# A Fourier filter with a sparse mixture of experts: padded first transform, batch 0 in thirds, new issue thresholds, a third list tile

## The chip, the cores and the metric

The kernel runs on one core of a Trainium2 chip. The metric is device microseconds of one execution. The engines are PE (TensorE, with its weight loads shown as PEld), DVE (VectorE), ACT (ScalarE), POOL (GpSimd) and SP (SyncE, which only issues DMA transfers here). ACT and POOL issue transfers too.

## The reference, cut to what matters

```python
X = np.fft.rfft(x, axis=1)                  # x: 8 x 2496 x 256
Yr = Xr @ w_r - Xi @ w_i + b_r              # 256 x 256 weights, on every frequency
Yi = Xr @ w_i + Xi @ w_r + b_i
Y = sign(Y) * max(|Y| - 0.01, 0)            # on real and imaginary part apart
y = np.fft.irfft(Y, n=2496, axis=1)         # 19968 tokens of 256

logits = y @ w_gate                         # 8 experts
expert = argmax(logits); gate = softmax(logits)[expert]
for each expert: keep the 80 tokens with the largest gate
    out[tok] = gate * (relu(y[tok] @ w1[e]) @ w2[e])      # 256 -> 1024 -> 256
all other rows of out are 0
```

The biases are drawn eight times larger than in the listing's distribution; nothing else hangs on that.

## The kernel before

**Transform.** 2496 is taken as 39 x 64. A token index is `64 a + n`, and the first transform (`stageA`) runs over the 39 values of `a`. Three values of `n` share one matmul, so the tile `xt` of loaded input has 39 x 3 = 117 partitions, and the weight `t1s` is a 117 x 117 block matrix (`t1f` is the same in fp32). A batch has six groups `q` of `stageA`, loaded in three chunks. Where `cut` holds, the input is split by `halve` into two fp16 parts `xs` (ACT at L286, POOL at L287) and multiplied at L301. Elsewhere the fp32 input is multiplied directly at L303. Each PSUM result is copied into `zs` as two fp16 parts (ACT at L318, DVE at L319) and stored in DRAM (L325). For batch 0 the store has two halves, 63 and then 54 rows: the first is issued at once and the second waits in the list `second`. Groups 3 to 5 of batch 0 use tiles named `YO` in the place of `zs`.

**Second transform and weights.** `loadZ` (L352) reads z back with another layout, `stageB` (L363 to L365) does the 64-point transform and copies it to `XT` (ACT L368, DVE L369). Stage C (L421) multiplies by the packed weights `WM` of 288 or 337 columns, then comes the soft threshold: ACT's `tp` (L445, or L432 in batch 7), DVE's `R` (L449, or L436), POOL's sums (L452). Then ACT, POOL and DVE make `YT` (L466 and L467, or L495 and L496). After that come the back transforms (L523 and L524 to `YO`, L577 to `hs`) and gate logits `G`.

**Lists.** From the gate values the kernel makes lists of tokens for each expert in three groups `g` (L868 to L915): group 0 and group 1 while the batches run, group 2 at the end. Two int32 tiles hold the lists, `tok` for groups 0 and 2 and `tokb` for group 1. Each is cleared by a memset (L915), filled, and written to the DRAM tensor `cid` (L893). Then rows are gathered, the experts run, and the result is scattered to `out`, which is cleared through the whole run (`out<-zero`, L264).

**Order.** Sixteen steps (batch, column half `ch`) are interleaved: while stage C of one step runs, `doA` puts groups of `stageA` of a later batch and `doB` the `stageB` of the next step in between. A scheduler sets the final order on each engine. `pin` and `keep` keep an instruction's program order, and `tc.issue_after(i)` forbids an instruction to stand ahead of `i`. Every engine then runs its own list strictly in order, so an instruction that waits holds up all behind it. Transfers take one of eight semaphore lanes in turn, and each waits for the previous transfer of its lane.

**Start.** Weights `w_r` and `w_i` come in and `consts` makes `WM` of them (ACT L212, DVE L213 and L214). The biases come by two transfers of 4-byte elements into `bt` (L233), and DVE makes `thr` of them (L235). When the six groups of batch 0 are through, 56 matmuls on zeros (L1376, "warm") stand on PE ahead of `stageB` of step (0, 0).

## Time and profile before

| | |
|---|---|
| three runs | 616.37, 613.64 and 617.41 us; median 616.37 |
| the profiled execution | 613.95 us, of which the span is 612.2 us |
| granted TensorE clock, mean | 0.947 of full speed |
| PE busy | 543.1 us (89%) |
| DVE busy | 400.3 us (65%) |
| POOL busy | 372.4 us (61%) |
| ACT busy | 324.0 us (53%) |
| DMA | 134.98 MB, mean 220 GB/s |

The profiled execution lies 2.4 us under the median of the runs and 0.3 us above the fastest. Times below are microseconds from the start of its span. "Busy" of PE counts matmuls that stand back to back, and a clock of 0.50 in a stretch means that each took twice as long as at 1.00. A row's idle time in brackets is that of its engine just ahead of the row, with what ended it.

### The profile page before, as it was taken

Reading aid. Unit: us, or ns where it says so; the run is one execution under the profiler, and the core shown is the slowest. Engines: PE = TensorE matmul, PEld = TensorE weight load, DVE = VectorE, ACT = ScalarE, POOL = GpSimd, SP = SyncE. Lnnn points to the kernel's source line nnn. Section 1 sums busy time; section 2 is a strip of 40 time slices with the busy share of each in tenths; the row PEclk is TensorE's granted clock in tenths of the full one; section 3 lists DMA queues with packets and bytes.
Section 4 is the critical chain, followed back from the end, with each engine's and each line's share of the span. In section 5 each row is a group of like instructions: output and inputs, shape, how many; then the busy total and the mean of one; then the engine's idle time right before and its main releaser. Section 6 shows DMA issues by size and latency. Waiting matters only on the chain. (4 is left out here: it accounts for less than half of the span.)

```text
span 612.2 us, 12947 instructions
## 1 busy us (share of the span) xinstructions
PE 543.1 (89%) x5059; PEld 396.4 (65%) x5059; DVE 400.3 (65%) x778; ACT 324.0 (53%) x466; POOL 372.4 (61%) x287
## 2 busy tenths in 40 slices
PE   7997599999999999999999859989889978987792
PEld 2464377767677876877786538757757766537692
DVE  3422445666767667666767936788898856846870
ACT  2314657576756656576665426555644547602571
POOL 2005767586867677776777636577752379465671
PEclk9899889999999999999999979989899958987987
DMA  6688697888699798978978884989834859648731
GB/s 191 218 256 202 215 230 237 234 256 239 202 286 257 211 254 253 300 201 242 248 253 235 251 229 90 286 248 283 236 99 117 270 179 319 186 140 281 253 100 32
DMA packets 97218, 134.98 MB, mean 220 GB/s; under 512 B 26547, under 2 KB 78274, under 8 KB 95396
## 3 DMA queue, kind: packets, MB, share of 16 engines
q1 hardware_dynamic: 88517, 113.94, 64.3%
q10 hardware_dynamic: 6506, 10.89, 5.9%
q0 software_dynamic: 2128, 9.25, 4.6%
q8 instruction: 42, 0.69, 0.5%
q14 instruction: 25, 0.20, 0.1%
HBM read 70.74 MB, written 63.31 MB: 219 GB/s over the span
## 5 line engine op out<-in xcount | busy, mean ns | idle before, releaser
L421 PE MATMUL ps<-XT,WM 128*128 128x288 f16 (+4 forms) x1536 | 222.8, 303 | 17.6 <-DVE R L449 12.2
L421 PEld LDWEIGHTS <-WM 128*128 128x128 f16 x1536 | 151.6, 100 | 78.1 <-issue 17.8
L287 POOL TENSOR_TENSOR xs<-xt,xs 117x1024 f16<-117x1024 f32 (+1 forms) x39 | 76.2, 1955 | 43.6 <-ACT xs L286 43.5
L449 DVE SCALAR_TENSOR_TENSOR R<-ps,thr,tp 128x674 f32<-128x674 f32 (+1 forms) x56 | 48.4, 866 | 76.6 <-ACT tp L445 69.7
L467 POOL TENSOR_TENSOR YT<-R,YT 128x1408 f16<-128x1408 f32 (+1 forms) x28 | 73.4, 2620 | 35.4 <-ACT YT L466 30.9
L445 ACT ACTIVATE tp<-ps,thr 128x674 f32<-128x674 f32 (+1 forms) x56 | 43.4, 778 | 85.2 <-PE ps L421 85.2
L452 POOL TENSOR_TENSOR R<-R,sgs 128x576 f32<-128x576 f32 x28 | 35.8, 1280 | 59.4 <-DVE R L449 56.6
L369 DVE TENSOR_TENSOR XT<-ps,XT 128x640 f16<-128x640 f32 (+2 forms) x64 | 51.5, 814 | 22.6 <-ACT XT L368 21.9
L319 DVE TENSOR_TENSOR zs<-ps,zs 117x1024 f16<-117x1024 f32 (+1 forms) x45 | 51.0, 1135 | 21.5 <-ACT zs L318 21.2
L363 PE MATMUL ps<-t2s,z 128*128 128x128 f16 x320 | 57.0, 220 | 6.3 <-DVE XT L369 3.7
L365 PE MATMUL ps<-t2s,z 128*128 128x128 f16 x320 | 57.1, 220 | 0.0
L364 PE MATMUL ps<-t2s,z 128*128 128x128 f16 x320 | 57.1, 220 | 0.0
L368 ACT ACTIVATE XT<-ps 128x640 f16<-128x640 f32 (+2 forms) x64 | 44.4, 701 | 21.8 <-PE ps L365 20.9
L301 PE MATMUL ps<-xs,t1s 117*117 117x512 f16 x213 | 52.6, 381 | 0.8 <-DVE zs L319 0.4
L318 ACT ACTIVATE zs<-ps 117x1024 f16<-117x1024 f32 (+1 forms) x45 | 42.8, 955 | 12.4 <-PE ps L301 6.2
L535 DVE TENSOR_TENSOR YO<-ps,YO 128x768 f16<-128x768 f32 (+1 forms) x50 | 45.3, 907 | 6.0 <-ACT YO L534 6.0
L577 PE MATMUL ps<-YO,vqs 128*128 128x512 f16 (+1 forms) x252 | 48.8, 334 | 0.0
L466 ACT ACTIVATE YT<-R 128x1408 f16<-128x1408 f32 (+1 forms) x28 | 35.4, 1266 | 22.3 <-POOL R L463 20.2
L286 ACT ACTIVATE xs<-xt 117x1024 f16<-117x1024 f32 (+1 forms) x39 | 38.3, 982 | 15.7 <-DMA xt<-in_x 15.7
L523 PE MATMUL ps<-wgi,YT 128*128 128x144 f16 (+1 forms) x302 | 43.5, 229 | 3.3 <-DVE R L449 1.5
L524 PE MATMUL ps<-wgi,YT 128*128 128x136 f16 (+1 forms) x302 | 42.9, 226 | 2.1 <-DVE YT L496 2.1
L534 ACT ACTIVATE YO<-ps 128x768 f16<-128x768 f32 (+1 forms) x50 | 38.6, 775 | 7.5 <-PE ps L524 5.7
(309 smaller groups left out, 1000.4 us busy)
## 6 DMA issues: line engine op xcount, KB each, us to landing
out<-zero SPq DMA_DIRECT2D x48, 384.0 KB
hd<-hs SPq DMA_DIRECT2D x94, 192.0 KB
xt<-in_x SPq DMA_DIRECT2D x44, 312.0 KB
zd<-zs SPq DMA_DIRECT2D x28, 468.0 KB
z<-zd SPq DMA_DIRECT2D x16, 528.0 KB
z<-zd SPq DMA_DIRECT2D x16, 432.0 KB
wt<-in_moe_w ACTq DMA_DIRECT2D x10, 512.0 KB
pair<-in_moe_w SPq DMA_DIRECT2D x8, 512.0 KB
```

The lines of the kernel that those rows point to most:

```text
L287: nc.gpsimd.tensor_tensor(xs[:, 1, :ng], xt[:, j0:j0 + ng], xs[:, 0, :ng], op=ALU.subtract)
L301: nc.tensor.matmul(pt[:117, 512 * j:512 * j + 512], t1s[:, t], xs[:, h, 2 * j:2 * j + 2], start=(i == 0), stop=(i == 2))
L319: nc.vector.tensor_tensor(zs[:, :ng, 1, :], pv[:117, :ng], zs[:, :ng, 0, :], op=ALU.subtract)
L363: nc.tensor.matmul(o, zz(0), t2s[:, cl, 0, :], start=True, stop=False)
L364: nc.tensor.matmul(o, zz(0), t2s[:, cl, 1, :], start=False, stop=False)
L365: nc.tensor.matmul(o, zz(1), t2s[:, cl, 0, :], start=False, stop=True)
L369: nc.vector.tensor_tensor(ov(1), pv, ov(0), op=ALU.subtract)
L421: nc.tensor.matmul(pt[:, o:o + e - a], WM[:, dh, m, wh, 128 * eh:128 * eh + 128], XT[:, dh, xh, c, a:e], start=(i == 0), stop=(i == len(te ...
L449: nc.vector.scalar_tensor_tensor(fv(Rf), pv, thr[:, eh, ri, 1:2], fv(t), op0=ALU.add, op1=ALU.min)
L467: nc.gpsimd.tensor_tensor(yv(1), rv, yv(0), op=ALU.subtract)
L535: dvs.append(nc.vector.tensor_tensor(yol, yy, yoh, op=ALU.subtract))
L577: nc.tensor.matmul(o, tab[:, v], yo(h), start=(i == 0), stop=(i == 2))
```

## The change

1. **Padding.** `t1` gets zero columns, so that the first transform gives 128 rows, with the two halves at 0 to 63 and 64 to 127. All tiles and stores of z have 64 or 128 rows for 63, 54 or 117.
2. **Batch 0.** The input chunks of batch 0 are thirds of `n`, and its z lies in three DRAM tiles. The first third of z is read back after group 3; the rest as before after the last group. The first input chunk of batch 1 is loaded by ACT's queue after group 1, where SP's queue loaded it after the second stores. 44 warm matmuls stand where 56 stood.
3. **Biases.** They are loaded as four rows of 128, transposed on PE, and `thr` is made from PSUM.
4. **Thresholds.** The operations that make `WM` are kept behind the last copies of z of batch 0. `halve` is kept behind the third last (batches 0 and 1) or the last (group (2, 0)) of the ACT instructions listed in `evA`, which are the copies of `stageA` and `stageB` and the `tp` of stage C. A new `split` is called behind the `doB` of the first step.
5. **Batch 7.** The memset of 30 PSUM columns stands behind ACT's `tp`, where it stood ahead of it.
6. **Lists.** Group 2 has a tile of its own, `tokc`.

```diff
-        "t1": split(np.kron(Fw[:, ROWS], np.eye(3)), 1),
+        "t1": split(np.insert(np.kron(Fw[:, ROWS], np.eye(3)), [63] + [117] * 10, 0.0, 1), 1),
-    zd = [[(dr.tile([k, 48, 512], F16, ...), dr.tile([k, 18, 512], F16, ...)) for c, k in enumerate(ZROWS if b == 0 else (39,))] for b in range(B)]
+    zd = [[[dr.tile([r, n, 512], F16, ...) for i, n in enumerate((8, 8, 6) if b == 0 else (16, 6))] for c, r in enumerate((64, 64) if b == 0 else (128,))] for b in range(B)]
...
     def consts():
-        for m, wt in enumerate(wraw):
-            nc.scalar.activation(WM[:, :, m, 0, :], wt, AF.Copy, scale=WS)
-            nc.vector.scalar_tensor_tensor(WM[:, :, m, 1, :], wt, WS, WM[:, :, m, 0, :], op0=ALU.mult, op1=ALU.subtract)
-        nc.vector.tensor_scalar(WM[:, :, 2], WM[:, :, 1], -1.0, None, op0=ALU.mult)
+        with tc.issue_after(evA[-1].ins), tc.issue_after(evD[-1].ins):
+            for m, wt in enumerate(wraw):
+                nc.scalar.activation(WM[:, :, m, 0, :], wt, AF.Copy, scale=WS)
+                nc.vector.scalar_tensor_tensor(WM[:, :, m, 1, :], wt, WS, WM[:, :, m, 0, :], op0=ALU.mult, op1=ALU.subtract)
+            nc.vector.tensor_scalar(WM[:, :, 2], WM[:, :, 1], -1.0, None, op0=ALU.mult)
...
+        bt = wkc.tile([4, 128], F32, name="bt")
         for r, bb in enumerate((b_r, b_i)):
-            bt = wkc.tile([128, 2], F32, name="bt", bufs=2)
-            nc.gpsimd.dma_start(bt, bb.rearrange("(h p) -> p h", p=128))
+            nc.gpsimd.dma_start(bt[2 * r:2 * r + 2], bb.rearrange("(h p) -> h p", p=128))
+        pt = psum()
+        nc.tensor.transpose(pt[:, 0:4], bt, ident[:4, :4])
...
-        nc.scalar.activation(xs[:, 0, :ng], xt[:, j0:j0 + ng], AF.Copy)
+        with tc.issue_after(evA[-3 if b < 2 else -1].ins) if b < 2 or (b, q) == (2, 0) else ExitStack():
+            nc.scalar.activation(xs[:, 0, :ng], xt[:, j0:j0 + ng], AF.Copy)
...
-        for i in parts:
-            p, e, m = ((0, 96, 48), (96, 128, 16))[i]
+        pieces = ((0, 48, 24), (48, 96, 24), (96, 128, 16)) if b == 0 else ((0, 96, 48), (96, 128, 16))
+        for i in parts or range(len(pieces)):
+            p, e, m = pieces[i]
...
-            if c0:
-                nc.vector.memset(pw[:, :c0], 0.0)
             acts.append(nc.scalar.activation(t[:, c0:], pw[:, c0:], AF.Relu, bias=thr[:, eh, ri, 0:1]))
+            if c0:
+                nc.vector.memset(pw[:, :c0], 0.0)
...
-        tok = const.tile([128, 2, 8, 4], I32, name="tokb" if g == 1 else "tok")
+        tok = const.tile([128, 2, 8, 4], I32, name=("tok", "tokb", "tokc")[g])
         nc.vector.memset(tok, 0)
...
+        if q == 1:
+            x1 = loadX(1, 0, None, (A_, A_, A_))
+        if q == 3:
+            z2 = loadZ(0, 0, None, (0,), False)
+    loadZ(0, 0, z2, (1, 2))
     pt = psum()
-    for _ in range(56):
+    for _ in range(44):
...
-            doC(0, 0); doC(0, 1); doA(); doC(1, 0); doA(); doC(1, 1); doA(4)
+            doC(0, 0); doC(0, 1); doA(); doC(1, 0); doA(); doC(1, 1); doA(4, False)
             for _ in Bl:
                 doB()
+            split()
```

How the change moves instructions is shown at three places. The first is **ACT from the last copies of batch 0's second transform on**, in the first step: `xs` is `halve`'s copy, `tp` the soft threshold's, `zs` and `XT` the copies of the first and second transform. Before:

```order
L368 ACTIVATE XT_185<-ps 128x2x320 x2
L286 ACTIVATE xs<-xt 117x1024 x2
L445 ACTIVATE tp_141<-ps,thr 128x674
L445 ACTIVATE tp_142<-ps,thr 128x674
L318 ACTIVATE zs<-ps 117x4x256
L445 ACTIVATE tp_141<-ps,thr 128x674
L466 ACTIVATE YT_435<-R 128x1408
L318 ACTIVATE zs<-ps 117x4x256
L445 ACTIVATE tp_142<-ps,thr 128x674
L318 ACTIVATE zs<-ps 117x4x256 x2
L286 ACTIVATE xs<-xt 117x512
```

After, the same stretch:

```order
L378 ACTIVATE XT_186<-ps 128x2x320 x2
L455 ACTIVATE tp_143<-ps,thr 128x674
L455 ACTIVATE tp_144<-ps,thr 128x674
L324 ACTIVATE zs<-ps 128x4x256
L455 ACTIVATE tp_143<-ps,thr 128x674
L477 ACTIVATE YT_428<-R 128x1408
L324 ACTIVATE zs<-ps 128x4x256
L290 ACTIVATE xs<-xt 117x1024
L455 ACTIVATE tp_144<-ps,thr 128x674
L290 ACTIVATE xs<-xt 117x1024
L324 ACTIVATE zs<-ps 128x4x256 x2
```

The two large `xs` copies have moved from ahead of all four `tp` to behind the third and behind the fourth. Some rows further on, the `xs` of group (2, 0) has moved from ahead of the first `XT` copy of the next step to behind all four of them.

The second place is **DVE just behind the last entries of the lists of group 0** (`G` is a sum of gate logits, `waits` names the queues that a row waits for; DMAHW is a transfer's lane). Before:

```order
L319 TENSOR_TENSOR zs<-ps,zs 117x4x256 [waits DMAHW7_49,Activation_49]
L629 TENSOR_REDUCE G<-Gs 128x160 [waits DVE_49]
L915 MEMSET tok 128x64 [waits DMAHW5_49,DVE_49]
L449 SCALAR_TENSOR_TENSOR R<-ps,thr,tp_142 128x674 [waits Activation_49]
L632 TENSOR_TENSOR gp<-G,gp 128x160 [waits Activation_49]
L319 TENSOR_TENSOR zs<-ps,zs 117x4x256 [waits DMAHW0_49,Activation_49]
```

After:

```order
L325 TENSOR_TENSOR zs<-ps,zs 128x4x256 [waits DMAHW3_49,Activation_49]
L640 TENSOR_REDUCE G<-Gs 128x160 [waits DVE_49]
L460 SCALAR_TENSOR_TENSOR R<-ps,thr,tp_144 128x674 [waits Activation_49]
L643 TENSOR_TENSOR gp<-G,gp 128x160 [waits Activation_49]
L325 TENSOR_TENSOR zs<-ps,zs 128x4x256 [waits DMAHW4_49,Activation_49]
```

The memset of the list tile, with its wait for a transfer, has gone from this place; the clearing of `tokc` stands at the start of DVE's list.

The third place is **SP's queue from the first stores of z on**, in batch 0 (`z_229` and `z_221` are the tiles that the second transform reads; the names of the DRAM tiles are `zd` and `ze` before, and `z_84` to `z_89` after). Before:

```order
L325 DMA zd_84<-zs 63x2048 x3
L325 DMA zd_84<-YO_212 63x2048
L325 DMA ze_85<-YO_212 63x2048
L325 DMA ze_85<-YO_224 63x1024
L352 DMA z_229<-zd_84 48x11x512 x2
L352 DMA z_229<-ze_85 16x11x512 x2
L325 DMA zd_86<-zs 54x2048 x3
L325 DMA zd_86<-YO_212 54x2048
L325 DMA ze_87<-YO_212 54x2048
L325 DMA ze_87<-YO_224 54x1024
L276 DMA xt<-in_x 39x2048 x6
```

After:

```order
L332 DMA z_84<-zs 64x2048 x2
L332 DMA z_85<-zs 64x2048
L362 DMA z_221<-z_84 24x11x512 x2
L332 DMA z_85<-YO_217 64x2048
L332 DMA z_86<-YO_217 64x2048
L332 DMA z_86<-YO_232 64x1024
L362 DMA z_221<-z_85 24x11x512 x2
L362 DMA z_221<-z_86 16x11x512 x2
L332 DMA z_87<-zs 64x2048 x2
L332 DMA z_88<-zs 64x2048
L332 DMA z_88<-YO_217 64x2048
L332 DMA z_89<-YO_217 64x2048
```

Two loads of the first third now stand between the third and the fourth store, and three of the six `xt` loads have left this queue for ACT's, where they stand between the copies to `zs` of groups 1 and 2.

## Rows read from the trace of the kernel before

**Rows 1.** The page's first part: busy time and share of the span, PE.

```profile
PE 543.1 (89%) x5059; PEld 396.4 (65%) x5059; DVE 400.3 (65%) x778; ACT 324.0 (53%) x466; POOL 372.4 (61%) x287
```

**Rows 2.** Stretches of the span, in microseconds: each row has the stretch and its length, the busy time of each engine with its instructions, the granted TensorE clock, the busy share of the DMA engines and GB/s.

```profile
28.00:35.00 7.00, 6.31 (x31) 2.73 (x29) 0.00 (x0) 0.00 (x0) 0.00 (x0) 1.00 0.92 245
...
76.00:80.00 4.00, 3.88 (x18) 2.46 (x18) 1.96 (x4) 1.62 (x3) 3.86 (x2) 0.50 0.79 283
...
96.00:340.00 244.00, 240.40 (x2247) 180.59 (x2245) 169.79 (x260) 157.97 (x219) 176.94 (x136) 1.00 0.84 245
...
354.00:362.00 8.00, 1.26 (x9) 0.70 (x8) 1.10 (x4) 2.89 (x4) 0.04 (x1) 0.88 0.95 256
362.00:366.00 4.00, 4.00 (x18) 2.42 (x18) 2.11 (x3) 0.00 (x0) 3.92 (x3) 0.50 0.47 154
...
485.00:508.00 23.00, 17.61 (x152) 13.80 (x149) 16.34 (x35) 9.73 (x13) 14.21 (x7) 0.63 0.74 229
508.00:540.00 32.00, 27.54 (x154) 17.27 (x151) 24.02 (x96) 19.71 (x26) 19.46 (x10) 0.95 0.72 223
```

**Rows 3.** The timeline of PE over the start: start, length, operation and tiles, count, and in brackets the idle time ahead of it with what ended it.

```profile
10.05 1.95 PE L303 MATMUL ps<-xt,t1f 117*117 117x512 f32 x4 [0.44 <-DMA XT<-in_x]
14.21 5.39 PE L303 MATMUL ps<-xt,t1f 117*117 117x512 f32 x8 [2.21 <-DMA xt<-in_x]
...
22.01 12.25 PE L1376 MATMUL ps<-z 128*128 128x512 f16 x56
34.95 0.22 PE L363 MATMUL ps<-t2s,z 128*128 128x128 f16 x1 [0.69 <-DMA z<-ze]
```

**Rows 4.** The timeline of DVE, over the last copies of batch 0's first transform.

```profile
21.97 0.68 DVE L213 SCALAR_TENSOR_TENSOR WM<-tp,WM 128x512 f16<-128x512 f32 x1
...
23.71 0.42 DVE L214 TENSOR_SCALAR WM<-WM 128x1024 f16<-128x1024 f16 x1
24.04 0.68 DVE L319 TENSOR_TENSOR YO<-ps,YO 117x512 f16<-117x512 f32 x1
```

**Rows 5.** The timeline of ACT there. The first row is the copy of group 2, the second those of groups 4 and 5.

```profile
16.91 1.02 ACT L318 ACTIVATE zs<-ps 117x1024 f16<-117x1024 f32 x1 [1.18 <-PE ps L303]
...
21.35 1.51 ACT L318 ACTIVATE YO<-ps 117x1024 f16<-117x1024 f32 x2
```

**Rows 6.** The timeline of SP: start and length of the issues of transfers.

```profile
25.20 1.36 SPq L352 DMA_DIRECT2D z<-zd  x2
27.57 1.22 SPq L352 DMA_DIRECT2D z<-ze  x2
...
34.30 5.97 SPq L276 DMA_DIRECT2D xt<-in_x  x6
```

**Rows 7.** Transfers issued between 8 and 36 us: tiles, queue, count, and KB of each.

```profile
z<-zd SPq DMA_DIRECT2D x2, 528.0 KB
...
z<-ze SPq DMA_DIRECT2D x2, 176.0 KB
```

**Rows 8.** The timeline of ACT in the first step.

```profile
47.91 1.06 ACT L286 ACTIVATE xs<-xt 117x1024 f16<-117x1024 f32 x1 [8.38 <-DMA xt<-in_x]
51.94 1.06 ACT L286 ACTIVATE xs<-xt 117x1024 f16<-117x1024 f32 x1 [2.97 <-DMA xt<-in_x]
52.90 1.52 ACT L445 ACTIVATE tp<-ps,thr 128x674 f32<-128x674 f32 x2
...
71.70 1.06 ACT L286 ACTIVATE xs<-xt 117x1024 f16<-117x1024 f32 x1 [3.87 <-DMA xt<-in_x]
72.67 0.69 ACT L368 ACTIVATE XT<-ps 128x640 f16<-128x640 f32 x1
```

**Rows 9.** The timeline of DVE in the first step.

```profile
53.74 1.75 DVE L449 SCALAR_TENSOR_TENSOR R<-ps,thr,tp 128x674 f32<-128x674 f32 x2 [13.32 <-ACT tp L445]
```

**Rows 10.** The timeline of PE in the first step.

```profile
54.71 1.97 PE L303 MATMUL ps<-xt,t1f 117*117 117x512 f32 x4 [3.54 <-DVE R L449]
...
69.14 0.22 PE L363 MATMUL ps<-t2s,z 128*128 128x128 f16 x1 [1.47 <-DVE zs L319]
...
74.26 0.26 PE L363 MATMUL ps<-t2s,z 128*128 128x128 f16 x1 [3.68 <-DVE XT L369]
```

**Rows 11.** The timeline of DVE behind the lists of group 0.

```profile
360.96 0.11 DVE L915 MEMSET tok<- 128x64 int32 x1 [6.90 <-DMA cid<-tok]
```

**Rows 12.** The timeline of PE: 24 matmuls of stage C with 288 columns, in an undisturbed place and behind that wait.

```profile
132.75 3.10 PE L421 MATMUL ps<-XT,WM 128*128 128x288 f16 x24
...
361.93 5.53 PE L421 MATMUL ps<-XT,WM 128*128 128x288 f16 x24 [6.74 <-DVE R L449]
```

**Rows 13.** The timeline of SP ahead of that wait.

```profile
353.61 1.27 SPq L352 DMA_DIRECT2D z<-ze  x2
354.97 0.54 SPq L893 DMA_DIRECT2D cid<-tok  x1
```

**Rows 14.** The timeline of ACT in batch 7.

```profile
490.53 1.06 ACT L826 ACTIVATE pair<-pair 128x1024 f16<-128x1024 f32 x1 [4.68 <-DMA pair<-in_moe_w]
491.49 1.36 ACT L495 ACTIVATE YT<-R 128x1408 f16<-128x1408 f32 x1
```

**Rows 15.** The waits from 430 to 500 us: engine and line, what it waited for, microseconds in all, times, the longest.

```profile
ACT tp L432 <- DVE ps L431: 9.4, 3, 3.9
...
DVE R L436 <- ACT tp L432: 1.2, 2, 0.9
```

More of the change, by code (lines that the diff above doesn't have):

```diff
@@ L148, in fourier_mix_then_moe @@
     zaq = stacks[4].enter_context(tc.tile_pool(name="zaq", bufs=1, side="right"))
[L149 removed]
+    zd = [[[dr.tile([r, n, 512], F16, name=f"z{i}{b}{c}") for i, n in enumerate((8, 8, 6) if b == 0 else (16, 6))] for c, r in enumerate((64, 64) if b == 0 else (128,))] for b in range(B)]
     hd = [dr.tile([B * 64 * 3, (7 - p) * 256], F32, name=f"hd{p}") for p in range(2)]
@@ L270, in loadX @@
         if c < 2:
-            parts = [(s, 0, 16 * s + 8 * c, 8) for s in range(3)]
+            parts = [(s, 0, 16 * s + 8 * c if b else 24 * c + 8 * s, 8) for s in range(3)]
         else:
-            parts = [(0, 0, 48, 6), (1, 0, 54, 6), (2, 0, 60, 4), (2, 4, 58, 2)]
+            parts = [(s, 0, 46 + 6 * s, 6) for s in range(3)]
         for i, (s, j, n, m) in enumerate(parts):
@@ L1313, in preX, with split, doA @@
             xls.append((a, loadX(*a)))
-    def doA(n=1):
-        for _ in range(n):
+    def split():
+        if Aq:
+            if cut(*Aq[0][:2]):
+                halve(*Aq[0])
+        elif xls:
+            (b, c), xt = xls[0]
+            if cut(b, 2 * c):
+                halve(b, 2 * c, xt)
+    def doA(n=1, last=True):
+        for k in range(n):
             if not Aq:
```

67 lines of the change are left out of this document (34 added, 33 removed).

## The prediction

> **What bounds the kernel now.** I read the page's first part, then the stretches of the span, then the timelines of the engines where PE sits idle. PE is busy 89% of the span [rows 1]. From 96 to 340 us it is busy 240.40 of 244.00 us at full clock, with the DMA engines at 0.84 [rows 2]: there PE is the bound, each engine runs its list in order, and a microsecond won earlier is handed on whole. What ACT and DVE save inside that stretch counts for nothing. PE loses time in four other places. At the start its first matmul of the second transform comes at 34.95, and the 56 warm matmuls ahead of it do no useful work [rows 3]. In the first step it waits 3.54, 1.47 and 3.68 us [rows 10], and after the last of these it runs 4 us at a clock of 0.50 [rows 2]. At 355 to 362 it waits 6.74 us, and the 24 matmuls that follow take 5.53 us where 24 of the same shape take 3.10 [rows 12]. From 430 on chains through ACT and DVE set the pace.
>
> **Term 1, the start: -2.7 us.** The matmul at 34.95 waited 0.69 us for `z<-ze`, the last part of z to be read back [rows 3]. Those loads are issued from 25.20 on [rows 6], behind the last store, which waits for DVE's last copy at 24.04 [rows 4]. The change shortens this chain twice. First, the operations for `WM` leave DVE: 0.42 us stood right ahead of the last copy, and 0.68 us ahead of the one before it [rows 4]. That earlier copy needs ACT's result, at about 22.4 (21.35 and two thirds of 1.51 [rows 5]), so of its 0.68 little is won. The saving is 0.42 to 1.10; I take 0.5, near the low end because ACT's copy sets it. Second, behind the last store 1408 KB were read (two of 528, two of 176 [rows 7]). The first third is 24 of 64 positions, 528 KB, and goes ahead. At the 245 GB/s of 28 to 35 us [rows 2] that is 2.2 us. Sum 2.7, so the second transform starts at 32.3. The 44 warm matmuls end at 22.01 + 44 x 12.25 / 56 = 31.6: a gap of 0.6 us, about today's 0.69, and the point below which the start cannot fall, -3.3.
>
> Three things can move this. ACT now issues three loads of batch 1's input ahead of the copy of group 2. An issue costs about 1.0 us (5.97 for six [rows 6]); the copy had 1.18 us of idle time ahead of it [rows 5], so up to 1.8 us is not covered there. I take 0, since the copies of groups 4 and 5 come more than 3 us later and set the end. The same loads move three times 312 KB, the size that the six issues also had, or 3.8 us at 245 GB/s, in a stretch where z is being stored. At worst 1.8 + 3.8 = 5.6 is lost, and the term is +2.9. The other way, PE waited 0.44 and 2.21 us for input at 10 and 14 us [rows 3]; if the short rows of the biases stood in the way of that input, their end would bring up to 2.65 more, -5.9 in all. No row prices them, so I take nothing.
>
> The Trainium skill ("DMA: Bandwidth & Descriptors", in "Why a DMA increments its semaphore by 16 and not by 1") speaks against the thirds: a transfer goes to the largest number of engines up to 16 that divides the slowest dimension of both sides, so a load of 24 rows uses 12 engines where one of 48 used 16. By that rule the second third would take 16/12 of 2.2 us and the term would be -2.0. No row here shows which engines carry a transfer.
>
> The padding itself costs PE nothing, since columns and counts of its matmuls stay, and it costs ACT and DVE nothing, since their copies keep their length per partition. The stores grow by 128/117: about 0.25 MB on 2.6 MB a batch (117 rows of 22 KB), 1.0 us of DMA work a batch at 245 GB/s. The 16% of DMA time that is free from 96 to 340 hides it. Without that cover it would be up to 1 us a batch, of which I leave 0 to +3 for the whole. The transpose of the biases is one short matmul next to the warm ones, and the six operations for `thr` and the displaced ones for `WM` go into the 7 us from 28 to 35 in which ACT and DVE do nothing [rows 2], ahead of the first use of both: nothing.
>
> **Term 2, the first step: -8.1 us.** On ACT an `xs` copy waits 8.38 us for input until 47.91 and a second one 2.97 until 51.94; the `tp` of stage C stands behind them and starts at 52.90 [rows 8]. DVE waits 13.32 us for that `tp` [rows 9], and PE 3.54 for DVE to free PSUM [rows 10]. In the new order all this goes on without the `xs`: the two copies stand behind the third and fourth `tp`. So 3.54 go. The second case is alike: the `xs` at 71.70 waited 3.87, the `XT` copy stands behind it [rows 8], and PE idles 3.68 until 74.26 [rows 10] and then runs at half clock, 3.88 us busy in 76 to 80 [rows 2], of which half, 1.9, is lost. The new order has this `xs` behind the `XT` copies, so 3.68 + 1.9 go as well. The wait of 1.47 hangs on a copy of `zs` that no edit moves, and stays. Sum 9.1. What is late next is the input itself: the fourth `xs` still waits for it and now stands just ahead of its own matmuls, so I give back one `xs`, 1.06 us [rows 8], and take -8.1. Bounds: only the first wait goes, -3.5; all three go, -10.6.
>
> **Term 3, the list tile: -6.9 us.** DVE's memset of `tok` waits 6.90 us until 360.96 for the transfer to `cid` [rows 11]. Behind it in DVE's list is the `R` for which PE waits 6.74 us [rows 12]. With a third tile that row is gone from there and at the start of the list nothing waits for it. The clock comes back too: 5.53 - 3.10 = 2.4 us. At most 9.2. But the loads of z for the next second transform were issued up to 354.88, just ahead of the `cid` transfer [rows 13], which landed at 360.96 or shortly before; the DMA engines were at 0.95 from 354 to 362, and have slack (0.47) only in 362 to 366 [rows 2]. The second transform follows the 24 matmuls. PE stood still from 361.93 - 6.74 = 355.2 [rows 12], so it would now come at about 355.2 + 3.1 = 358.3, and z may land up to 2.6 us later, near 360.9. I take 2.3 of that as lost, since the transfers are issued by the same queue in the same order: -6.9. Bounds: -9.2 if z is there in time, -4.5 if the new wait of 2.6 also halves the clock for some 4 us.
>
> **Term 4, batch 7: +0.5 us.** ACT's `tp` waited 9.4 us in three places for DVE's memset, while DVE waited only 1.2 for `tp` [rows 15]: at most 1.2 is won. Against it, ACT's list in batch 7 is rearranged. Before, one weight copy that waited 4.68 stood ahead of `YT` [rows 14]; now two weight copies and a `tp` stand there. At 1.06 for a copy and 0.7 for a `tp` this is up to 1.8 us, or more if the second waits for its own transfer. I take +0.5, from -1.2 to +2.4.
>
> **The sum.** 613.95 - 2.7 - 8.1 - 6.9 + 0.5 = 596.75 for an execution like the profiled one. That one lies 2.4 us under the median of the three runs, so I add half of it: **598 us**.
>
> **Rivals.** (a) New waits take the place of the old: in the first step only the first stall goes (-3.5), and behind the list the z loads are late at half clock (-4.5). For it speaks that DMA is at 0.95 there [rows 2]; against it that the new order puts nothing that waits ahead of `tp`. 613.95 - 2.7 - 3.5 - 4.5 + 0.5 + 1.2 = 605. (b) The start is lost: ACT's three issues and their bytes delay the copies and stores, term 1 at +2.9, 603.6. (c) The change does not do what it says: the input is what is late, and the wait only moves from ACT to PE, with nothing won at the start. Then terms 1 and 2 are zero: 613.95 - 6.9 + 0.5 + 1.2 = 608.8, and 611.2 with term 3 at -4.5. For it speaks that each of the `xs` waits ends with a transfer [rows 8]; against it that the input of batch 1's first chunk comes earlier. (d) Slower: in batch 7 the second weight copy ahead of `YT` waits for its transfer as long as the first, 4.68 + 1.06 + 0.7 = 6.4 us [rows 14]. PE's clock, 0.63 from 485 to 508 [rows 2], then stays at its lower level (1.2 of 2.4 GHz) through the next stretch, whose 27.54 us of PE work at 0.95 [rows 2] would take 52 at 0.50, 20 us more than the 32 there. 598 + 6.4 + 20 = 624. It decides only if PE waits go on recurring up to 540. Against it: DVE still has its own work during that wait.
>
> **How the numbers follow.** Forecast 0.60, (a) 0.22, (b) 0.07, (c) 0.08, (d) 0.03. The range of 8 in 10 reaches from 588 (all four terms at their best ends: 613.95 - 5.9 - 10.6 - 9.2 - 1.2 + 1.2) to 610, which holds (a), (b) and part of (c). About 1% (610.2 and 622.5) is what a measurement of this kernel can tell from no change. Faster by more: the forecast, (a), (b) and the better half of (c), less 0.04 for sizes that I have wrong, 0.89. Slower: (d), 0.03. The rest 0.08.
>
> **What would show it.** In the profile after: the first matmul of the second transform near 32 with a gap under 1 us; `tp` of the first step right behind the `XT` copies, and no PE wait over 1.5 us from 35 to 80; no DVE wait for `cid`, full clock behind it, and a PE wait of about 2 us for `z`; from 430 on the same length as before, within 2 us. I am wrong if PE waits for `xt` or `xs` in the first step, if DMA nears 1.0 from 96 to 340, or if the stretch from 485 to 540 is much longer.

## The result, and the profile after

The changed kernel takes **594.75 us** (four runs, 592.45 to 595.72) where the kernel before took 616.89 on the same chip. The ratio is 0.9637, with a 95% interval from 0.958 to 0.969. The forecast was 598 us, range 588 to 610. The profiled execution took 594.34 us, of which the span is 592.5, so 19.7 us less span than before. Executions over 1.5% above the fastest of their kernel are left out of the ratios but not of the medians, and the profiled one of memset_order_alone (623.84 us) is such a one.

PE's share is as high as before [rows 1], and it is busy for 7.7 us less, of which the 12 warm matmuls that were left out make 2.6:

```profile
PE 535.4 (90%) x5047; PEld 388.4 (66%) x5048; DVE 403.9 (68%) x778; ACT 324.2 (55%) x466; POOL 372.4 (63%) x287
```

The stretches of the span that answer to [rows 2], from the start to the middle (engines, clock, DMA share, GB/s in the same order):

```profile
28.00:35.00 7.00, 1.53 (x8) 0.55 (x6) 0.49 (x6) 0.00 (x0) 0.00 (x0) 0.87 0.70 203
...
36.00:40.00 4.00, 3.44 (x33) 3.47 (x34) 0.48 (x1) 0.81 (x1) 0.00 (x0) 0.50 1.00 234
...
76.00:80.00 4.00, 3.65 (x38) 2.89 (x36) 2.09 (x3) 3.50 (x5) 3.45 (x2) 1.00 0.94 237
...
96.00:320.00 224.00, 220.67 (x2051) 161.50 (x2050) 153.35 (x229) 143.53 (x199) 162.93 (x123) 1.00 0.85 255
```

The start is worse than before: PE does nothing for most of 28 to 35 us, and from 36 to 40 its clock is at 0.50. From 76 to 80 the clock is back, and the middle is bound by PE as it was.

**Where the time went.** Stage C has 1536 matmuls, in the same order in every kernel here, and the start of the n-th of them in PE's timeline is a clock that all share. The table gives it for the kernel before, and for every other kernel how much earlier (-) or later (+) it comes. No. 1 is the first of step (0, 0), No. 97 the first of the second step (each of the 16 steps has 96), No. 289 stands in the undisturbed middle, No. 1033 and No. 1081 are ahead of and behind the place of the list stall, No. 1393 and the last lie in batch 7, which begins with No. 1345 (448.0 us before, 16.8 earlier in the changed kernel). The last column is what follows the last one: lists, gathers, experts, scatter.

| us | No. 1 | 97 | 289 | 1033 | 1081 | 1393 | last | end of span | behind the last |
|---|---|---|---|---|---|---|---|---|---|
| before | 38.63 | 76.12 | 132.75 | 348.30 | 372.78 | 464.85 | 486.74 | 612.17 | 125.4 |
| changed | +3.3 | -6.9 | -7.7 | -7.9 | -15.6 | -19.7 | -18.6 | -19.7 | 124.3 |
| changed_again | +3.2 | -7.2 | -8.0 | -8.1 | -15.8 | -19.9 | -18.9 | -14.9 | 129.4 |
| thresholds_alone | -1.7 | -9.1 | -9.8 | -10.2 | -13.5 | -12.8 | -12.8 | -15.6 | 122.6 |
| list_tile_alone | +3.7 | +1.2 | +1.5 | +1.2 | -8.1 | -5.6 | -5.6 | -3.5 | 127.5 |
| memset_order_alone | +1.1 | +1.4 | +2.1 | +1.8 | +2.4 | +0.5 | +1.6 | +9.9 | 133.8 |
| start_alone | +3.7 | +0.8 | +0.8 | +0.4 | -8.7 | -6.3 | -6.3 | -4.7 | 127.0 |
| padding_alone | +0.3 | -3.0 | -2.7 | -3.0 | -11.7 | -10.3 | -10.3 | -7.2 | 128.5 |
| shared_list_tile | +4.3 | -5.8 | -6.6 | -6.9 | -14.6 | -19.7 | -18.6 | -15.1 | 128.8 |
| memset_undone | +1.6 | -8.6 | -9.3 | -9.5 | -17.3 | -17.7 | -17.7 | -15.6 | 127.5 |
| first_third_on_ACT | 0.0 | -10.1 | -10.9 | -11.1 | -18.9 | -20.4 | -19.3 | -12.0 | 132.7 |
| thirds_all_late | +1.6 | -8.7 | -9.5 | -9.6 | -17.3 | -21.1 | -20.0 | -16.8 | 128.7 |
| input_late_on_SP | -1.0 | -8.7 | -9.5 | -9.6 | -17.2 | -19.3 | -18.2 | -16.4 | 127.3 |
| start_reordered | +0.1 | -10.1 | -10.9 | -11.2 | -18.9 | -20.7 | -19.8 | -22.5 | 122.8 |

Read along the row of the changed kernel: it loses 3.3 us at the start, wins 11.0 by No. 289 (10.2 of them in the first step), keeps that to 0.2 us through 215 us of PE-bound middle, wins 7.7 at the lists, 1.3 from there to batch 7, 1.8 in batch 7, and 1.1 behind the last matmul. The four parts of the forecast were -2.7, -8.1, -6.9 and +0.5.

**The start.** PE's timeline, answering to [rows 3]:

```profile
13.61 3.70 PE L307 MATMUL ps<-xt,t1f 117*128 117x512 f32 x8 [2.55 <-DMA xt<-in_x]
...
19.72 9.66 PE L1394 MATMUL ps<-z 128*128 128x512 f16 x44
...
36.56 0.27 PE L373 MATMUL ps<-t2s,z 128*128 128x128 f16 x1 [7.03 <-DMA z<-zs]
...
41.90 7.35 PE L431 MATMUL ps<-XT,WM 128*128 128x337 f16 x48
```

The last group is done 2.3 us earlier than before (19.72 against 22.01), since it and the group ahead of it begin 0.6 us earlier and eight matmuls take 3.70 us where they took 5.39 [rows 3]. The wait for input ahead of them is still 2.55 us, where it was 2.21, so the new biases did not shorten it. Yet the second transform begins 1.6 us later, behind 7.03 us of waiting for z, and then needs 41.90 - 36.56 = 5.3 us up to the first stage C matmul, where it took 38.63 - 34.95 = 3.7 before: the gap costs half the clock too. SP's timeline shows why z is late, answering to [rows 6]:

```profile
19.56 0.45 SPq L332 DMA_DIRECT2D z<-zs  x1
23.32 1.69 SPq L362 DMA_DIRECT2D z<-z  x2
25.10 2.23 SPq L332 DMA_DIRECT2D z<-YO  x3
29.77 3.04 SPq L362 DMA_DIRECT2D z<-z  x4
```

The two loads of the first third waited until 23.32 for stores to land. The three last stores stood behind them and were issued from 25.10 on, though DVE had finished the last of their copies by 22.4. The loads of the other thirds followed at 29.77, where the loads of all z began at 25.20 before.

ACT's timeline shows the price of the early input there:

```profile
13.58 3.62 ACTq L279 DMA_DIRECT2D xt<-in_x  x3
17.25 1.02 ACT L324 ACTIVATE zs<-ps 128x1024 f16<-128x1024 f32 x1 [3.38 <-DMA xt<-in_x]
```

ACT issues the three loads until 17.20 and only then copies group 2, though PE was through with that group at about 15.5 (half of the eight matmuls at 13.61).

**The first step.** ACT, answering to [rows 8]:

```profile
48.03 0.82 ACT L455 ACTIVATE tp<-ps,thr 128x674 f32<-128x674 f32 x1 [5.24 <-PE ps L431]
49.33 0.82 ACT L455 ACTIVATE tp<-ps,thr 128x674 f32<-128x674 f32 x1 [0.47 <-PE ps L431]
...
60.46 1.05 ACT L290 ACTIVATE xs<-xt 117x1024 f16<-117x1024 f32 x1
```

The `tp` wait for PE alone, and `xs` for nothing. On PE the waits of 3.54, 1.47 and 3.68 us [rows 10] have shrunk to this one and two of 0.32 and 0.35; the 1.47, which the prediction kept, is gone with the others:

```profile
64.14 1.46 PE L305 MATMUL ps<-xs,t1s 117*128 117x512 f16 x6 [0.84 <-POOL xs L291]
```

**The lists.** PE, answering to [rows 12]; the first row is the step ahead of the old stall, the second that of the stall:

```profile
340.43 5.28 PE L431 MATMUL ps<-XT,WM 128*128 128x337 f16 x24 [2.73 <-DVE R L460]
...
348.80 3.10 PE L431 MATMUL ps<-XT,WM 128*128 128x288 f16 x24
```

The stall of 6.74 us is gone, clock included. The wait of 2.73 ahead of it was there before as well, but then the 24 matmuls behind it ran at full clock and now they take 5.28:

```profile
348.30 3.64 PE L421 MATMUL ps<-XT,WM 128*128 128x337 f16 x24 [2.75 <-DVE R L449]
```

### The profile page after: what moved, and what is told of

It reads as the page before. It is cut to its first block, busy times and chain, and to the rows that moved or that the text cites. A ratio compares the mean times of both kernels' runs of the same rounds, so it can differ in the third digit from the quotient of the medians.

```text
span 592.5 us, 12919 instructions
## 1 busy us (share of the span) xinstructions
PE 535.4 (90%) x5047; PEld 388.4 (66%) x5048; DVE 403.9 (68%) x778; ACT 324.2 (55%) x466; POOL 372.4 (63%) x287
## 5 line engine op out<-in xcount | busy, mean ns | idle before, releaser
L431 PE MATMUL ps<-XT,WM 128*128 128x288 f16 (+4 forms) x1536 | 221.0, 301 | 10.2 <-DVE R L460 4.7
L325 DVE TENSOR_TENSOR zs<-ps,zs 128x1024 f16<-128x1024 f32 (+1 forms) x45 | 51.1, 1136 | 20.8 <-ACT zs L324 20.5
L373 PE MATMUL ps<-t2s,z 128*128 128x128 f16 x320 | 58.1, 223 | 7.5 <-DMA z<-zs 7.0
L374 PE MATMUL ps<-t2s,z 128*128 128x128 f16 x320 | 58.1, 223 | 0.0
L375 PE MATMUL ps<-t2s,z 128*128 128x128 f16 x320 | 58.1, 223 | 0.0
L305 PE MATMUL ps<-xs,t1s 117*128 117x512 f16 x213 | 52.6, 379 | 1.0 <-POOL xs L291 0.8
L324 ACT ACTIVATE zs<-ps 128x1024 f16<-128x1024 f32 (+1 forms) x45 | 42.9, 954 | 14.6 <-PE ps L305 6.4
L588 PEld LDWEIGHTS <-vqs 128*128 128x128 f16 x252 | 24.8, 100 | 22.4 <-issue 2.1
```

Source lines behind the costliest of these rows:

```text
L305: nc.tensor.matmul(pt[:, 512 * j:512 * j + 512], t1s[:, t], xs[:, h, 2 * j:2 * j + 2], start=(i == 0), stop=(i == 2))
L325: evD.append(nc.vector.tensor_tensor(zs[:, :ng, 1, :], pv[:, :ng], zs[:, :ng, 0, :], op=ALU.subtract))
L373: nc.tensor.matmul(o, zz(0), t2s[:, cl, 0, :], start=True, stop=False)
L374: nc.tensor.matmul(o, zz(0), t2s[:, cl, 1, :], start=False, stop=False)
L375: nc.tensor.matmul(o, zz(1), t2s[:, cl, 0, :], start=False, stop=True)
L431: nc.tensor.matmul(pt[:, o:o + e - a], WM[:, dh, m, wh, 128 * eh:128 * eh + 128], XT[:, dh, xh, c, a:e], start=(i == 0), stop=(i == len(te ...
```

## The experiments

**Does each part carry its term?** Four kernels make one part each.

thresholds_alone, the kernel before with the issue thresholds and `split`:

```diff
+        with tc.issue_after(evA[-3 if b < 2 else -1].ins) if b < 2 or (b, q) == (2, 0) else ExitStack():
             nc.scalar.activation(xs[:, 0, :ng], xt[:, j0:j0 + ng], AF.Copy)
...
-            doC(0, 0); doC(0, 1); doA(); doC(1, 0); doA(); doC(1, 1); doA(4)
+            doC(0, 0); doC(0, 1); doA(); doC(1, 0); doA(); doC(1, 1); doA(4, False)
+            split()
```

> The kernel before with the issue thresholds and the later split alone (start, padding, lists and memset as before). Theory: the xs copies behind the tp and XT copies are what frees the first step, so PE's waits of 3.54 and 3.68 us and the half clock go: 8 to 10 us, about 607 us. Rival: the input of batch 1 is what is late; without its earlier load PE waits for xs itself and only 3.5 us or less are won, 613 us or more.

Measured: 600.46 us against 618.57 of the kernel before beside it, ratio 0.969 (0.960 to 0.978). By No. 289 it is 9.8 us ahead, 1.7 of them at the start. The input comes no earlier here, and the first step is still shorter by 8.1 us. So the order on ACT is what held the first step up, and the rival falls. The 1.7 at the start may in part be the displaced `WM` operations; two executions of one kernel agree there to 0.1 (changed and changed_again), but kernels whose code at the start is that of the kernel before also lie at +1.1 (memset_order_alone), so a microsecond there is not evidence. The whole is better than expected, since 3.3 us more are won at the lists, with the old tile and the old stores; the memset waits half as long there:

```profile
347.10 0.11 DVE L920 MEMSET tok<- 128x64 int32 x1 [3.24 <-DMA cid<-tok]
```

list_tile_alone:

```diff
-        tok = const.tile([128, 2, 8, 4], I32, name="tokb" if g == 1 else "tok")
+        tok = const.tile([128, 2, 8, 4], I32, name=("tok", "tokb", "tokc")[g])
```

> The kernel before with one edit: group 2 of the lists has its own tile. Theory: the wait of 6.90 us and the half clock behind it go, and nothing else moves, so the stage C matmuls behind the lists come 6 to 9 us earlier (in the changed kernel this stretch gave 7.7) and the whole is 608 to 611 us. Rival: the 7.7 us of the changed kernel came from how its earlier stream met the z loads; alone the edit runs into those loads and gives 4.5 us or less, 612 to 613 us.

Measured: 612.30 us, ratio 0.990 (0.982 to 0.997). From No. 1033 to No. 1081 it wins 9.3 us, all that the stall had cost (9.2 by the prediction's working), and z is not late. The whole lies above the expected 608 to 611 and in the rival's range all the same, since it began 3.7 us later at No. 1. The scheduler had put two operations for `WM` ahead of a copy of z on DVE, which ends the last copy at 25.4 us for 24.7, and the second transform waited 4.57 us for z; what made the rest of the delay was not traced.

start_alone, the changed kernel without thresholds, list tile and memset order:

> The changed kernel with thresholds, list tile and memset order undone: padding, thirds, long bias rows, the early load of batch 1 and 44 warm matmuls remain. Theory: the first stage C matmul comes 3.3 us later than before, as in the changed kernel, and the earlier input gives some of it back in the first step: in all 616 to 620 us. Rival: the start by itself is a gain and it is the thresholds that delay it in the changed kernel; then the first stage C matmul comes 2 to 3 us earlier than before and the whole is 613 to 615 us.

Measured: 605.98 us, ratio 0.976 (0.969 to 0.983), better than both expectations. The start is as late as in the changed kernel (+3.7) and most of it comes back in the first step. What nobody expected is 9.1 us at the lists, without the new tile. The memset still waits for the list transfer, but for 0.24 us.

memset_order_alone:

```diff
-            if c0:
-                nc.vector.memset(pw[:, :c0], 0.0)
             acts.append(nc.scalar.activation(t[:, c0:], pw[:, c0:], AF.Relu, bias=thr[:, eh, ri, 0:1]))
+            if c0:
+                nc.vector.memset(pw[:, :c0], 0.0)
```

> The kernel before with one edit: in batch 7 the memset of 30 PSUM columns stands behind ACT's tp. The changed kernel won 4.1 us between 390 and 465 us that the prediction did not see. Theory: this edit is the cause, so alone it wins 3 to 4 us there, 613 us. Rival: those 4 us come from another meeting of weight transfers and matmuls after the shift of everything ahead; then this edit alone moves the stretch by less than 1 us, 616 to 617 us.

Measured: 618.36 us, ratio 1.002 (0.997 to 1.008). From No. 1081 to No. 1393 it wins 1.9 us, and 0.8 by the last matmul. Neither expectation fits well, and in the whole time nothing is to be seen. Inside batch 7 the edit shows more clearly: from No. 1345 to No. 1393 it wins 2.9 us (memset_undone, below).

**Two cures for one stall.** The stall at the lists went without the tile in start_alone, so something in the start edits reaches 300 us further on. The next two kernels ask which.

padding_alone is the kernel before with 128 rows in the first transform and in the stores of z, and three transfers for the last input chunk:

```diff
-        "t1": split(np.kron(Fw[:, ROWS], np.eye(3)), 1),
+        "t1": split(np.insert(np.kron(Fw[:, ROWS], np.eye(3)), [63] + [117] * 10, 0.0, 1), 1),
...
-            for ch, p in enumerate((slice(0, 63), slice(63, 117)) if b == 0 else (slice(0, 117),)):
+            for ch, p in enumerate((slice(0, 64), slice(64, 128)) if b == 0 else (slice(0, 128),)):
```

> The kernel before with 128 rows in the first transform and in all stores of z, and the last chunk of input in three transfers, nothing else. Theory: the wider stores let the DMA engines and SP's queue run ahead, so the list transfer is through in time and the stretch behind the lists comes 7 to 9 us earlier, with less than 2 us at the start: 607 to 611 us. Rival: it is the earlier input or the thirds of batch 0 that shifted SP's queue; then padding by itself leaves the wait at 5 us or more, 615 us or more.

Measured: 610.00 us (ten runs), ratio 0.990 (0.986 to 0.994). It wins 3.0 us by the second step, where less than 2 was expected, and 8.7 at the lists, so the other cure is in this kernel. DVE's memset there, answering to [rows 11]:

```profile
351.70 0.11 DVE L920 MEMSET tok<- 128x64 int32 x1 [0.68 <-DMA cid<-tok]
```

SP had issued the z loads that stand ahead of the list transfer earlier in the program:

```profile
341.47 3.93 SPq L357 DMA_DIRECT2D z<-z  x4
348.74 0.40 SPq L898 DMA_DIRECT2D cid<-tok  x1
```

Before, the same loads and the list transfer were issued so:

```profile
350.32 3.24 SPq L352 DMA_DIRECT2D z<-zd  x2
353.61 1.27 SPq L352 DMA_DIRECT2D z<-ze  x2
354.97 0.54 SPq L893 DMA_DIRECT2D cid<-tok  x1
```

Measured from matmul No. 1033 (348.30 before, 345.29 here), they come 3.8 us ahead of it, where they came 2.0 behind it before: SP's queue runs 5.8 us earlier against PE. The stretch from No. 289 to No. 1033 holds the same PE work in both, first in the kernel before and then in this one:

```profile
132.75:348.30 215.55, 210.13 (x1982) 158.78 (x1980) 154.43 (x253) 137.50 (x191) 157.25 (x120) 1.00 0.85 246
```

```profile
130.06:345.29 215.23, 210.09 (x1982) 154.72 (x1980) 154.32 (x253) 137.28 (x191) 157.26 (x120) 1.00 0.88 258
```

The DMA engines move 258 GB/s there instead of 246, though PE sets the pace in both (256 to 258 in every kernel with the padding, 246 to 250 in those without). Of the 2.6 MB that this makes, 1.0 MB is the padding itself (25 stores); the rest is that SP's queue gets through sooner. The Trainium skill ("DMA: Bandwidth & Descriptors", in "Why a DMA increments its semaphore by 16 and not by 1") would point to the stores: by its rule a store of 117 rows runs on 13 engines and one of 128 on 16. That the number of engines is the cause no row shows.

A rival stands untested. Every kernel with the padding, the changed one among them, also loads the last chunk of each batch's input in three transfers where four stood, and SP's lead over PE begins there. At the four issues of `hd` just ahead (118.98 before, 116.29 here) SP is 2.7 us earlier, as PE is; behind the input it is 3.5 us earlier. First before, then here:

```profile
127.34 3.28 SPq L276 DMA_DIRECT2D xt<-in_x  x4
130.72 1.30 SPq L352 DMA_DIRECT2D z<-ze  x2
```

```profile
124.67 2.49 SPq L275 DMA_DIRECT2D xt<-in_x  x3
127.26 1.30 SPq L357 DMA_DIRECT2D z<-z  x2
```

Four such chunks lie between 96 and 300 us, so by an estimate from these rows up to 4 x 0.8 = 3.2 of the 5.8 us could come from them. The kernel shows that the padding, with this transfer left out, lets the queue run ahead; how much of it is the wider stores stays open.

shared_list_tile is the changed kernel with the tile's edit undone:

```diff
-        tok = const.tile([128, 2, 8, 4], I32, name=("tok", "tokb", "tokc")[g])
+        tok = const.tile([128, 2, 8, 4], I32, name="tokb" if g == 1 else "tok")
```

> The changed kernel with group 2 of the lists back in group 0's tile. With padding and the other start edits but the shared tile, the wait for the list transfer was 0.24 us where it was 6.90 before. Theory: the changed kernel has two cures for one stall, so taking the tile's cure away costs less than 1.5 us at the stage C matmuls behind the lists, 594 to 597 us. Rival: the cures add, and the 7 us of the single edit come back, 601 to 603 us.

Measured: from No. 1033 to No. 1081 it wins 7.7 us, as the changed kernel does; the memset waits for nothing at all:

```profile
347.09 0.11 DVE L926 MEMSET tok<- 128x64 int32 x1
```

At the last matmul it is level with the changed kernel. The whole was 599.79 us, ratio 0.976 (0.970 to 0.983), 2.8 us above the theory's range and under the rival's; the difference to the changed kernel's profile lies entirely behind the last matmul, 128.8 us against 124.3, which the run of the changed kernel below explains. So the tile was worth nothing beside the start edits, the padding among them.

memset_undone is the changed kernel with the memset ahead of `tp` again, the reverse of the diff above.

> The changed kernel with batch 7's memset ahead of ACT's tp again. Three kernels without the new order gained 1 to 3 us less by the end of stage C than behind the lists, and the one with that order alone gained 1.9 more. Theory: the new order is worth 4 to 6 us between 390 and 465 us here, 597 to 601 us. Rival: the changed kernel's gain there is from other meetings of transfers; then the stretch changes by under 1.5 us, 594 to 596 us.

Measured: 601.13 us, ratio 0.979 (0.973 to 0.986). From No. 1081 to the last it wins 0.4 us, the changed kernel 3.0 (4.1 up to No. 1393). But first_third_on_ACT, which has the new order, wins 0.4 there too: ahead of batch 7 the kernels gain or lose 1 to 2 us whatever the order. Batch 7 by itself is clear. From No. 1345 to No. 1393 all eight kernels with the new order win 2.9 us on the kernel before; of the five without it, thresholds_alone wins nothing and the others lose 1.5 to 1.7. To the last matmul the changed kernel wins 1.8 there and memset_undone loses 1.5. So the order is worth 3.3 us, somewhat under the theory's 4 to 6, and the rival falls. The profile of before shows what it removes. PE waits 2.25 us for `gr`, a result of the gate weights that DVE makes late (so it does in memset_undone):

```profile
456.36 0.57 DVE L765 TENSOR_TENSOR gr<-ps,gq 78x256 f32<-78x256 f32 x1
...
460.92 0.08 DVE L431 MEMSET ps<- 128x30 f32 x1 [2.61 <-PE ps L421]
```

```profile
457.08 0.33 PE L771 MATMUL ps<-ident,gr 78*128 78x78 f32 x2 [2.25 <-DVE gr L765]
```

In the changed kernel the scheduler has `gr` ahead of the copies to `hs`, PE has no such wait, and the memset waits for `tp` instead:

```profile
436.96 0.59 DVE L776 TENSOR_TENSOR gr<-ps,gq 78x256 f32<-78x256 f32 x1
...
442.98 0.08 DVE L442 MEMSET ps<- 128x30 f32 x1 [2.07 <-ACT tp L440]
```

About 1 us of the 2.9 is lost again behind No. 1393, in the eight kernels with the new order alone. There DVE's `gp`, which splits the gate logits into fp16 parts, now begins while POOL is at `YT`, and takes 2.32 us where it takes 0.30 in memset_undone; behind it PE waits for `R`. Rows of the three engines in the changed kernel, and then the `gp` of memset_undone, where POOL was through with `YT` at 457.75:

```profile
457.24 2.85 POOL L507 TENSOR_TENSOR YT<-R,YT 128x1408 f16<-128x1408 f32 x1 [11.82 <-ACT YT L506]
457.95 2.32 DVE L643 TENSOR_TENSOR gp<-G,gp 128x160 f16<-128x160 f32 x1
462.37 6.04 PE L431 MATMUL ps<-XT,WM 128*128 128x320 f16 x48 [0.81 <-DVE R L448]
```

```profile
458.40 0.30 DVE L643 TENSOR_TENSOR gp<-G,gp 128x160 f16<-128x160 f32 x1
```

**What costs 3.3 us at the start?** Four kernels change the changed kernel's start alone. All are read at the first matmul of the second transform (36.56 in the changed kernel, 35.44 in its second run, 34.95 before) and at No. 1. memset_undone has the instructions of the start in the same order as the changed kernel on every engine; it comes at 35.08, and at No. 1 at +1.6. So executions of one and the same start differ by 1.5 us there, and each of the four below was profiled once.

first_third_on_ACT and thirds_all_late both take the two early loads out of SP's queue, the one to ACT behind its last copy, the other behind the last store:

```diff
-        if q == 3:
-            z2 = loadZ(0, 0, None, (0,), False)
-    loadZ(0, 0, z2, (1, 2))
+    z2 = loadZ(0, 0, None, (0,), eng=nc.scalar)        # first_third_on_ACT
+    loadZ(0, 0, z2, (1, 2))
...
+    z2 = loadZ(0, 0)                                   # thirds_all_late
```

> The changed kernel with the two loads of the first third of z issued by ACT's queue behind its last copy of batch 0, where SP's queue issued them between the third and the fourth store. Theory: on SP they waited for a store to land and kept the three last stores back for 4 us or more, so the second transform comes at 31 to 33 us (36.56 in the changed kernel, 34.95 before), no half clock behind it, and the first stage C matmul 4 to 6 us earlier: 588 to 591 us. Rival: the transfers themselves are the limit there (batch 1's input lies among them); then the second transform stays at 35 us or later and the whole at 593 us or more.

> The changed kernel with all loads of the first z behind the last store on SP. Theory: reading the first third early on SP loses more by holding back stores than it wins, so the second transform comes earlier than the changed kernel's 36.56, at 33 to 35 us. Rival: reading early wins something even so, and it comes at 37 us or later.

input_late_on_SP puts batch 1's first input back where it was:

```diff
-        if q == 1:
-            x1 = loadX(1, 0, None, (A_, A_, A_))
...
-        xls.append((Xq[0], loadX(*Xq.pop(0)) if k else x1))
+        xls.append((Xq[0], loadX(*Xq.pop(0))))
```

> The changed kernel with batch 1's first input back on SP behind the second stores. Theory: its 936 KB stood ahead of the stores of z, so the second transform comes 2 to 4 us earlier than 36.56, and the first step is no longer than in the changed kernel. Rival: the load costs nothing at the start, and without it the first step waits for that input: second transform at 36 us or later, first step 1 us or more longer.

start_reordered has the first third on ACT, that input behind it, and 58 warm matmuls:

```diff
+    z2 = loadZ(0, 0, None, (0,), eng=nc.scalar)
+    loadZ(0, 0, z2, (1, 2))
+    x1 = loadX(1, 0, None, (A_, A_, A_))
     pt = psum()
-    for _ in range(44):
+    for _ in range(58):
```

> The changed kernel with the first third of z issued by ACT behind its last copy, batch 1's first input issued by ACT behind those loads, and 58 warm matmuls. Theory: what delays the second transform is first the three stores held back on SP (3.2 us, seen) and then 936 KB of input moved ahead of them (up to 3.8 us); without both it starts at 29 to 31 us, PE has no gap, the clock stays, and the first stage C matmul comes at 33 to 35 us (41.90 in the changed kernel, 38.64 with the first third on ACT). The whole: 585 to 590 us if the stretch at the end is as short as in the changed kernel. Rival: the loads themselves, not what is ahead of them, take the time; then it starts at 33 us or later and the first stage C matmul comes at 37 us or later.

The first matmul of the second transform in PE's timeline, in the order first_third_on_ACT, thirds_all_late, input_late_on_SP, start_reordered:

```profile
33.49 0.27 PE L373 MATMUL ps<-t2s,z 128*128 128x128 f16 x1 [4.86 <-DMA z<-zs]
```

```profile
34.50 0.27 PE L373 MATMUL ps<-t2s,z 128*128 128x128 f16 x1 [5.35 <-DMA z<-z]
```

```profile
32.35 0.22 PE L373 MATMUL ps<-t2s,z 128*128 128x128 f16 x1 [3.65 <-DMA z<-zs]
```

```profile
33.38 0.22 PE L373 MATMUL ps<-t2s,z 128*128 128x128 f16 x1 [2.26 <-DMA z<-z]
```

Reading the first third early on SP wins nothing: with all loads late it is 34.50, 0.6 to 2.1 us earlier than in the three executions of the changed start, though at No. 1 (+1.6) level with memset_undone. That it is a loss, as the theory had it, is likely but not clear of that scatter. Issued by ACT the early third does win, 1.6 to 3.1 us against those three and 1.0 against all late. That is what the theory said in direction, but short of its 31 to 33, and No. 1 came 3.3 us earlier than in the changed kernel, at half clock, for 4 to 6 without it. The early input costs more, 2.7 to 4.2 us here. With it gone from ACT's queue, ACT copies group 2 at 14.80 for 17.25; the run takes the issues and the bytes away together and does not separate them. It is paid back in part: input_late_on_SP is 4.2 us ahead of the changed kernel at No. 1 and 1.8 at No. 97, because the first step then takes 2.4 us longer. start_reordered did not add the two: it began at 33.38, no better than first_third_on_ACT and 1.0 later than input_late_on_SP, and its No. 1 came at 38.69. Its theory falls, by the bounds that the rival named. But that it is the loads themselves, the rival's reason, is not shown: ACT issued the input while SP was still issuing the loads of the other two thirds, so its bytes now stood among those loads:

```profile
20.90 2.68 ACTq L279 DMA_DIRECT2D xt<-in_x  x3
```

```profile
21.17 6.86 SPq L362 DMA_DIRECT2D z<-z  x4
```

In all four kernels No. 1 follows 5.2 to 5.8 us behind the first matmul, where it takes 3.7 at full clock.

In the whole, first_third_on_ACT took 600.84 us (four runs; 588 to 591 was expected, and its stretch behind the last matmul is one of the longest, 132.7), thirds_all_late 599.01 and input_late_on_SP 596.63 (two runs each).

start_reordered took 596.31 us in the whole, ratio 0.965 (0.958 to 0.972), and the changed kernel beside it on the same chip 599.32, ratio 0.973 (0.967 to 0.978). The intervals overlap, and of the 2.9 us by which it leads that kernel at No. 97 only 0.9 are left at the last matmul. So it is no clear gain over the changed kernel.

**Is the end of the program the same length each time?** The changed kernel was run once more on the chip of the last three.

> The changed kernel once more, on the chip of the three kernels beside it. Behind the last stage C matmul it took 124.3 us; four kernels whose instructions there stand in the same order took 127.5 to 132.7, with a lower TensorE clock in that stretch. Theory: that length varies between executions and chips by some 5 us, whatever the kernel, so this one gives 594 to 600 us here. Rival: the variants' edits lengthen it; then this gives 593 to 596 us again and the stretch 124 to 125 us.

Measured: 599.32 us (six runs, 599.01 to 601.96). Up to the last stage C matmul its profiled execution agrees with the first one to 0.3 us; behind it, it took 129.4 us and not 124.3. The stretch in which they part, first the changed kernel and then its second run:

```profile
532.00:552.00 20.00, 14.73 (x261) 13.98 (x262) 14.85 (x37) 7.48 (x19) 13.86 (x16) 0.91 0.86 300
```

```profile
532.00:552.00 20.00, 11.13 (x145) 9.76 (x144) 10.24 (x29) 4.24 (x12) 10.50 (x11) 0.91 0.83 291
```

At the same clock and nearly the same DMA rate the second has done 145 matmuls where the first did 261: the gathers of the tokens' rows began 0.7 us later and were then held up longer. What sets this is open. The rival, that the variants' edits lengthen the end, falls with it. It makes whole times of these kernels uncertain by some 5 us, which is why the table's columns and not the medians carry the argument, and why the first ratio, 0.964, may flatter the change: the second is 0.973.

## Why the prediction was right, and where its steps were not

**The whole** came out 3.3 us under the forecast, and 1.3 above it in the second run. It did so partly by luck, since three of the four terms were off and the errors cancelled: against the forecast 6.0 us were missing at the start, 7.4 more were won from the first step to the last stage C matmul, and 1.1 behind it.

**Term 1, the start: -2.7 forecast, +3.3 measured** (+1.6 to +3.3 over three executions of that start). Rival (b) put the term at +2.9, and that is what happened. The main step that failed is the price of the early input. The prediction had 1.8 us for ACT's issues and 3.8 for bytes, but as an end of the range, and took 0, since the copies of groups 4 and 5 come later "and set the end" of the chain. They did not: z was late although DVE had ended those copies by 22.4 us. The input costs 2.7 to 4.2 us (input_late_on_SP), of which the shares of issues and bytes are open. The second step is that the first third "goes ahead" and wins 2.2 us of bytes. It won nothing (thirds_all_late): SP's own order was not followed, in which those loads wait for a store to land and three stores stand behind them. The gap under 1 us was forecast from the 44 warm matmuls; it became 7.0 and cost the clock as well, 1.6 us that the term did not hold.

**Term 2, the first step: -8.1 forecast, -11.0 measured, -8.1 with the thresholds alone.** The mechanism was right. The size is the outer bound (-10.6) and a little more, because the earlier input, which was charged to the start, returns 2.4 us here: in input_late_on_SP PE waits 0.68 and 1.13 us in the first step and its clock is at 0.60 from 60 to 64 us. The wait of 1.47, which was to stay, went. The one `xs` that I gave back, 1.06, was 0.84.

**Term 3, the lists: -6.9 forecast, -7.7 measured.** Right in size, but two of its steps were not. z was not late: PE goes from the 24 matmuls into the second transform without a wait. The 1.6 us that are missing from the full 9.2 went elsewhere, to the half clock behind the wait of 2.73. And the cause was named too narrowly. The padding, with the input transfer that goes with it, moves the list transfer out of the way, and with the changed start the tile is worth nothing (shared_list_tile); the thresholds by themselves halve the wait. I had set the padding at nothing, 0 to +3, on the ground that it adds bytes which idle DMA time hides. That step failed in its sign: padding_alone is about 6 us faster as a whole, 8.7 of them won at the lists.

**Term 4, batch 7: +0.5 forecast, -1.8 measured.** I asked what ACT and DVE wait for from each other, and found 1.2 us. I did not ask what else changes place on DVE when the memset does: `gr`, for which PE waited 2.25 us, and `gp`, which now runs beside POOL's `YT` and gives about 1 us back. The two weight copies ahead of `YT`, which the term charged and rival (d) feared, are not what holds it up there: that `YT` [rows 14] waits for DVE.

```profile
473.84 1.38 ACT L506 ACTIVATE YT<-R 128x1408 f16<-128x1408 f32 x1 [2.43 <-DVE R L498]
```

The stretch behind did not fall to half clock as (d) had it (0.88 from 490 to 520 us). The 1.3 us won between the lists and batch 7 are in no term; the other kernels with the same edits range there from 2.2 won to 1.3 lost, so they are no sure part of the change.

**Rivals (a) and (c).** In the first step no new wait of 1 us or more took the place of the old ones, and with the input no earlier the thresholds still won their 8.1 us, so (c) falls outright. Of (a) the half clock came, but ahead of the lists' place and not behind it.

## What to carry to other kernels

When a load is moved ahead of stores in an in-order queue, price what stands behind it while it waits, and not only the bytes that it takes out of the way. A stall that waits for a transfer has as many cures as there are reasons for the transfer to be late: before adding the gains of several edits, ask whether they end the same wait. A kernel that makes one part alone has to leave out all the rest: what rides along with the part stays a rival. A saving passes through a PE-bound middle to some tenths of a microsecond, so the start of a numbered matmul is a better clock for comparing kernels than the end of the program.

## What the runs showed of the hardware that I had not expected

Stores of 128 rows in the place of 117, with one input transfer fewer in each batch, went with 258 GB/s where 246 were moved in a stretch of 215 us with equal PE work, and made the kernel 1.0% faster, though it moves 2.0 MB more in all (136.96 for 134.98). DVE's `gp` took 0.30 us in all six profiled kernels in which POOL had ended `YT` before it began, and 2.0 to 2.4 in all eight in which `YT` was still running; in each of the eight it ended 0.2 us behind `YT`. PE's wait ahead of the second transform brought half the clock behind it after 2.26 us in one kernel (start_reordered, mean granted clock 0.68 from 33.38 us to No. 1) and not after 2.76 us in another (padding_alone, 1.00 and 3.7 us to No. 1), so the length of the wait by itself does not tell whether the clock falls:

```profile
35.25 0.22 PE L368 MATMUL ps<-t2s,z 128*128 128x128 f16 x1 [2.76 <-DMA z<-z]
```
